# A two-layer decode kernel: other pairs stay on the chip between the layers, attention loops that run to each layer's end with the softmax ahead of the values, and the constants loaded from another queue

## The chip, the cores and the metric

One core of a Trainium2 chip runs the whole program in one launch. The metric is the device time of one execution in microseconds (us). Five executions of the kernel before took 525.45 to 526.99 us, median 525.98 us.

The core has a matrix engine (PE; its weight loads are listed as PEld), a vector engine (DVE), a scalar engine (ACT) and a queue engine (SP) that issues transfers. Sixteen DMA engines carry every transfer from HBM into the on-chip memory. "Granted clock" is the share of full speed that PE was allowed.

## The reference

Two layers, each an attention over one query token and a gated MLP, with the same weights and the same key and value caches in both layers. Only the last 4096 positions of the caches are read (W below).

```python
x = x + A(layernorm(x)); x = x + B(layernorm(x))     # twice

def A(x):                    # 32 heads of 192, D = 640, W = 4096
    q = x @ wq               # 640 x 6144
    scores = q . k * 192 ** -0.5          # per head: 4096 scores
    o = softmax(scores) @ v
    return o @ wo            # 6144 x 640

def B(x):                    # F = 1536
    return (sigmoid(x @ w_gate) * (x @ w_up)) @ w_down
```

All inputs are bfloat16. Both layers read the same 32 heads of keys and values, so what stays on the chip at the end of the first layer need not be loaded again for the second.

## The kernel before, in words

**Units.** The heads are worked on in 16 pairs. For each pair there are two units of 3552 KB (28416 bytes on each of 128 partitions): unit A holds the pair's columns of wq and its keys, unit B its values and its rows of wo. The tile `big` has seven slots of one unit each (`NSLOT = 7`) and behind them a region for MLP weights, `mreg`. `A_SLOT[l][p]` and `B_SLOT[l][p]` say in which slot the units of pair p lie in layer l. The code counts layers from 0; in this text layer 1 is `l == 0` and layer 2 is `l == 1`.

**What stays.** `KEPT` lists the units that are not released at the end of layer 1: A and B of pairs 13, 14, 15, and A of pair 12. Layer 2 starts with these pairs. Pair 12's values are loaded a second time into `mreg` (items `va`, `vb`, `vc`), and its rows of wo (`wo12`) over its own A slot once `Q(12)` has read it. The other twelve pairs, 0 to 11, are loaded again.

**Order of loads.** `seq` is the list of all loads in the order in which SP issues them: A0, A1, B0, A2, B1, ... The last B unit of a layer is cut into three pieces (`b1`, then two `b0`). A load is written down by `prefetch()` as soon as its slot is free at that point of the program (`take`, `release`), and it waits on the chip for the last reader of that slot. SP works them off strictly in order. A slot of A is released after `QK`, a slot of B after `PVout`. In layer 1 the pairs 0 to 13 rotate through slots 0 to 3; slots 4, 5 and 6 are first used for pairs 14 and 15. The first transfer on SP is the small tile of constants and x (`cst`, item `x`).

**One step.** `step(p, prev)` works on the scores of pair p and the values of the pair before:

- `Q`: 15 small matmuls form the query (L350), DVE masks it into `qs` (L353).
- `QK`: 24 matmuls give the scores (L365).
- `soft`: DVE takes the maximum (L375), ACT spreads it into `diag` (L378), PE transposes and spreads it (L381), DVE forms the bias (L382, L384). The argument `mid` puts other work between `diag` and L381.
- `PVmm`: 32 matmuls of e with the values (L419), and two copies on ACT (L424).
- `PVout`: transposes (L434), the scaling on DVE (L437), 15 matmuls with wo (L444).
- `expo`: ACT computes e and its sum (L389). `ET`: e is transposed (L395, L399) and the reciprocal of the sum is formed (L400, L402, L404).

The order of PE before is Q, QK, PVmm(prev), L381, PVout(prev), ET. Each engine works in the order in which the operations are written down (`pg.op`). PE's part of steps 1 to 12 of layer 1 and of steps 2 to 9 of layer 2 is a loop on the chip whose body is two steps (`loop`); the other steps are written out. `emit_pe` builds the loop: a wait of the body counts up by a fixed number per turn. In the kernel before, the thresholds must fit exactly from the second turn on.

**MLP.** Layer 1's MLP loads gate and up weights into `mreg` in parts (`wg`, `u1`, `u2`), then the down weights (`d1`, `d2`) over parts that have been read, then `va`, `vb`, `vc`. Layer 2's MLP weights (`fg`, `fu`, `fd`) go to `mreg`, `U_SLOT` and `D_SLOT`; `finish` ends the program.

Of the kernel before, what the change touches and what calls it, by code (L numbers as in the profile page):

```python
# [17 lines left out]
NPAIR = H // 2  # L18
# [26 lines left out]
class _Prog:  # L45

    def __init__(self):
        self.ops = {e: [] for e in ("pe", "dve", "act", "pool", "dma")}
        self.cnt = {e: 0 for e in ("pe", "dve", "act", "pool")}
        self.dcnt = {}  # L50
        self.seg = None

    def op(self, eng, fn, rd=(), wr=(), ex=(), multi=False):
        d = {}

        def add(ev):
            if ev is not None and d.get(ev[0], 0) < ev[1]:
                d[ev[0]] = ev[1]
        for r in rd:
            add(r.w)  # L60
        for r in wr:
            if r.w is not None and r.w[0] != eng:
                add(r.w)
            for ev in r.rd:
                if ev[0] != eng:
                    add(ev)
        for r in ex:
            for e, ev in r.last.items():
                if e != eng:
                    add(ev)  # L70
        if eng == "pe":
            d.pop("pe", None)
            multi = True
        self.cnt[eng] += 1
        ev = (eng, self.cnt[eng])
        for r in rd:
            r.rd.append(ev)
        for r in wr:
            r.w = ev
            r.rd = []  # L80
        for r in ex:
            r.last[eng] = ev
        self.ops[eng].append(dict(fn=fn, deps=d, multi=multi, seg=self.seg))
        return ev

    def dma(self, fn, sem, wr=(), extra=()):
        d = {}

        def add(ev):
            if ev is not None and d.get(ev[0], 0) < ev[1]:  # L90
                d[ev[0]] = ev[1]
        for r in wr:
            for ev in r.rd or [r.w]:
                add(ev)
        for ev in extra:
            add(ev)
        self.dcnt[sem] = self.dcnt.get(sem, 0) + 16
        ev = ("d:" + sem, self.dcnt[sem])
        for r in wr:
            r.w = ev  # L100
            r.rd = []
        self.ops["dma"].append(dict(fn=fn, deps=d, sem=ev[0]))
        return ev
# [3 lines left out]
def decode_kernel(ctx: ExitStack, tc: tile.TileContext, cx: bass.AP, ua: bass.AP, ub: bass.AP,  # L107
# [75 lines left out]

    A_SLOT = [{p: p % 2 for p in range(NPAIR)}, {p: 3 if p % 2 == 0 else 2 for p in range(NPAIR)}]
    B_SLOT = [{p: 2 + p % 2 for p in range(NPAIR)}, {p: 5 if p % 2 else 0 for p in range(NPAIR)}]
    A_SLOT[0].update({14: 4, 15: 6})
    B_SLOT[0].update({14: 5, 15: 2})
    A_SLOT[1].update({0: 1, 1: 4, **{p: A_SLOT[0][p] for p in (12, 13, 14, 15)}})
    B_SLOT[1].update({0: 6, **{p: B_SLOT[0][p] for p in (13, 14, 15)}})
    KEPT = {(k, p) for p in (13, 14, 15) for k in "ab"} | {("a", 12)}  # L190
    U_SLOT, D_SLOT = 1, 4
    NHALF = NB * DH // 2
# [10 lines left out]
    seq += [("wg", 0), ("wg", 1), ("u1",), ("u2",), ("d1",), ("d2",), ("va",), ("vb",), ("vc",)]  # L203
    tail = stream(1, range(12))
    assert tail[0] == ("a", 1, 0)
    seq += [("a0", 0), ("a0", 1), ("wo12",)] + tail[1:]
    seq += [("fg",), ("fu",), ("fd", 0), ("fd", 1), ("fd", 2)]
    seq_pos = [0]
    busy = set()
    ev_done = {}  # L210
    halves = {(0, NPAIR - 1), (1, 11)}
    A0CUT = WQE + W
# [11 lines left out]
    def try_load(it):  # L224
# [17 lines left out]
        elif k == "a0":  # L242
            if f"a13_{it[1]}" not in ev_done:
                return False
            s = A_SLOT[1][0]
            o0, o1 = ((0, A0CUT), (A0CUT, UNIT))[it[1]]
            pg.dma(q_dma(slot(s, o0, o1 - o0), ua[0][:, o0:o1]), f"a0{it[1]}", wr=[res(f"a0{it[1]}")] + ([rslot[s]] if it[1] else []),
                   extra=[ev_done[f"a13_{it[1]}"]])
        elif k == "wg":
# [16 lines left out]
        elif k in ("va", "vb", "vc"):  # L266
            if "down0" not in ev_done:
                return False
            o0, o1 = MOFF[k[1]]
            pg.dma(q_dma(mreg(o0, o1 - o0), ub[12][:, o0:o1]), k, wr=[rm[k[1]]])  # L270
        elif k == "wo12":
            if "Q12" not in ev_done:
                return False
            pg.dma(q_dma(slot(A_SLOT[1][12], 0, WOE), ub[12][:, VE:UNIT]), "wo12", wr=[res("wo12")], extra=[ev_done["Q12"]])
        elif k == "fg":
# [23 lines left out]

    pg.dma(q_dma(cst[:, 0:CE], cx), "x", wr=[res("cst")])  # L300
    prefetch()
# [35 lines left out]
    def attention(l, xi):  # L337
# [6 lines left out]
        def Q(p, y):  # L344
            sa = A_SLOT[l][p]

            def f(t):
                for i, c0 in enumerate((0, P, 2 * P)):
                    for c in range(DC):
                        ins = t.matmul(qe[:, i:i + 1], lhsT=slot(sa, c * 2 * DH + c0, P), rhs=xq[:, c:c + 1], start=(c == 0), stop=(c == DC - 1))  # L350
                return ins
            ev = pg.op("pe", f, rd=[res("xq"), rslot[sa]] + ([res("a00")] if l == 1 and p == 0 else []), ex=[rb[3]])
            pg.op("dve", lambda v: v.tensor_tensor(out=qs[:, y], in0=qe[:, 0:3].unsqueeze(2).to_broadcast([P, 3, 32]), in1=mask3, op=ALU.mult),  # L353
                  rd=[res("cst")], wr=[res(f"qs{y}")], ex=[rb[3]])
            return ev

        def QK(p, y, x=0, ks=(0, 1, 2)):
# [3 lines left out]
            def f(t):  # L361
# [5 lines left out]
                return ins  # L367
            ev = pg.op("pe", f, rd=[res(f"qs{y}"), rslot[sa]] + ([res("a00"), res("a01")] if l == 1 and p == 0 else []), ex=sc_x[3:5])
            if ks[-1] == 2 and not (l == 0 and ("a", p) in KEPT) and not (l == 1 and p in (12, 13)):
                release(sa)  # L370
# [36 lines left out]
        def PVmm(p, z):  # L407
            inm = l == 1 and p == 12
            sv = None if inm else B_SLOT[l][p]
# [17 lines left out]
        def PVout(p, z):  # L427
            inm = l == 1 and p == 12
            sv = None if inm else B_SLOT[l][p]

            def tm(t):
                for c in range(3):
# [5 lines left out]
                  rd=[res(f"Rn{z}0"), res(f"Rn{z}1")], wr=[res("oTb")], ex=[rb[6]])  # L438
            wo = slot(A_SLOT[1][12], 0, WOE) if inm else slot(sv, VE, WOE)

            def im(t):
# [4 lines left out]
                return ins  # L446
            sa = A_SLOT[1][12]
            pg.op("pe", im, rd=[res("oTb")] + ([res("wo12"), rslot[sa]] if inm else [rslot[sv]]), ex=[rb[7]])
            if inm:
# [7 lines left out]

        def step(p, prev, y=0):
            Q(p, y)
            QK(p, y)  # L460
            soft(0, hook=None, mid=lambda: PVmm(prev, prev % 2))
            PVout(prev, prev % 2)
# [9 lines left out]
        if l == 0:  # L472
# [6 lines left out]
            ET(0)  # L479
            loop(0, 12)  # L480
            first, n = 12, NPAIR
        else:
            Q(13, 0)
            ln_sq(xi)
            mark("a13_0", QK(13, 0, ks=(0,)))
            mark("a13_1", QK(13, 0, ks=(1, 2)))
            Q(14, 1)
            ln_rstd(K2_ATT, eps_a, srs_c, res("srs"))
            mark("Q12", Q(12, 0))
            QK(14, 1, 1)  # L490
            soft(0, scale_pm)
            expo()
            ET(0)
            Q(15, 1)
            soft(1)
            expo(1)
            QK(15, 1)
            soft(0, mid=lambda: PVmm(13, 0))
            PVout(13, 0)
            ET(1)  # L500
            expo()
            PVmm(14, 1)
            ET(0)
            QK(12, 0)
            PVout(14, 1)
            soft(0, mid=lambda: PVmm(15, 0))
            PVout(15, 0)
            expo()
            ET(1)
            Q(0, 0)  # L510
            QK(0, 0)
            soft(0, mid=lambda: PVmm(12, 1))
            PVout(12, 1)
            expo()
            ET(0)
            step(1, 0)
            loop(1, 8)
            first, n = 9, 12
        for p in range(first, n - 1):
            step(p + 1, p)  # L520
        PVmm(n - 1, (n - 1) % 2)
        PVout(n - 1, (n - 1) % 2)
        return residual(xi)
# [113 lines left out]
    def emit(name, h, lo=0, hi=None, known=None):  # L637
        known = {} if known is None else known
        for o in pg.ops[name][lo:hi]:
# [7 lines left out]
            if att is not None:  # L647
                ins._wait_ge(S[att[0]], att[1])
            ins.then_inc(S[o["sem"]], 16) if name == "dma" else ins.then_inc(S[name], 1)
        return known  # L650

    def emit_pe(t):
        ops, known, i = pg.ops["pe"], {}, 0
        tmp = t.alloc_register("thr_tmp")
        while i < len(ops):
# [27 lines left out]
            for (p, k), d in vals.items():  # L683
                base[p, k] = max(v - it * step_of(p, k) for it, v in d.items())
                assert all(base[p, k] == v - it * step_of(p, k) for it, v in d.items() if it), ("wait threshold is not affine", p, k, d)
                if len(set(v - it * step_of(p, k) for it, v in d.items())) > 1:
                    print("first differs", seg, p, k, d, base[p, k])
            for it in range(len(its)):
# [21 lines left out]

    NFIRST = 3
    known_sp = emit("dma", nc.sync, 0, NFIRST)
    with nc.Block() as block:
        @block.sync
# [80 lines left out]
```

## Time and profile before

| | |
|---|---|
| median of five executions | 525.98 us |
| the profiled execution, whole | 525.18 us |
| its span, first to last instruction | 523.3 us |
| mean granted clock of PE | 0.592 |
| busy: PE, DVE, ACT | 280.4, 96.0, 87.9 us |
| read from HBM | 219.18 MB, 419 GB/s over the span |

A page of the profile cuts the span into 40 slices of 13.08 us and gives the DMA engines' busy share in tenths and their rate in GB/s for each. A chain of waits follows the work that ended last back to the start. A timeline lists instructions: start, duration, engine, line, what is written and read, and in brackets the idle time ahead of it with what ended it. A row of the windows gives, for a stretch of the span, each engine's busy time with the number of instructions, then the granted clock, the DMA share and the rate. The groups of PE's waits, each with total time, number of times and the longest, in us:

```profile
PE o L419 <- DMA big<-in_ub_dram: 110.1, 24, 5.0
PE bank L350 <- DMA big<-in_ua_dram: 46.0, 23, 8.8
PE bank L395 <- ACT e_sb L389: 21.4, 30, 2.0
PE bank L444 <- DVE sh L437: 15.2, 32, 0.6
PE bank L381 <- ACT diag L378: 3.5, 3, 2.0
```

Behind the page lie the trace's records of single DMA packets: start, duration, size and queue of each. One row of a unit, 28416 bytes, is one packet, and each of the 16 DMA engines carries 8 of a unit's 128 rows. When an engine has finished its share, it writes 4 bytes to the load's semaphore, so 16 such writes mark a load's landing; the time from the first to the last of them tells how far the engines are apart.

### The profile page before, as it was taken

The numbers are of one execution on the slowest core, as the hardware profiler recorded it, in microseconds if no ns is written. First come the engines' busy times: TensorE is split into PE (matmuls) and PEld (weight loads), VectorE is DVE, ScalarE is ACT, GpSimd is POOL, SyncE is SP. The second block draws the span as 40 slices with busy tenths as digits, with TensorE's granted clock in tenths as the row PEclk, the third lists the DMA queues.
The fourth block names the chain that finished last, engine by engine and source line by source line (L and its number), as shares of the span: only waits on it lengthen the run. The fifth ranks groups of instructions, "written<-read, shape, count | busy, mean of one in ns | idle before, by whom it ended". The sixth has DMA issues, their size and how long they took to land.

```text
span 523.3 us, 8405 instructions
## 1 busy us (share of the span) xinstructions
PE 280.4 (54%) x3716; PEld 144.8 (28%) x3716; DVE 96.0 (18%) x372; ACT 87.9 (17%) x171; POOL 0.2 (0%) x4
## 2 busy tenths in 40 slices
PE   0635455544635354544655668788455544645375
PEld 0222122212322122212224434444222212322234
DVE  1211121112111121112111232223121112111121
ACT  0121021201121021201121022312121201121120
POOL 0000000000000000000000000000000000000000
PEclk9995555555556655766665556766655555556655
DMA  8999999999999999999999999999999999999995
GB/s 350 421 440 426 434 428 432 434 426 434 428 434 431 430 432 430 434 430 431 427 411 370 366 434 437 425 434 431 426 430 432 433 432 430 428 433 429 420 424 220
DMA packets 11118, 219.50 MB, mean 419 GB/s; under 512 B 1368, under 2 KB 1368, under 8 KB 2904
## 3 DMA queue, kind: packets, MB, share of 16 engines
q1 hardware_dynamic: 11096, 219.19, 98.4%
q8 instruction: 16, 0.26, 0.2%
q14 instruction: 6, 0.05, 0.0%
HBM read 219.18 MB, written 0.00 MB: 419 GB/s over the span
## 4 chain that ended last, share of the span: by engine, by line
DMA 75%; PE 18%; DVE 3%; SPq 1%; ACT 1%; issue 1%; ACTq 0%; DVEq 0%
DMA big<-in_ub_dram 59%; DMA big<-in_wu_dram 8%; PE o L419 8%; DMA big<-in_wd_dram 8%; PE scores L365 3%; PE bank L381 2%; PE bank L444 2%; SPq L182 1%; ACT e_sb L389 1%; DVE sc L382 1%; PE bank L402 1%; PE bank L350 1%; DVE sc L384 1%; PE o L365 1%; DVE sc L375 0%
## 5 line engine op out<-in xcount | busy, mean ns | idle before, releaser
L419 PE MATMUL o<-big,et_sb 128*2 128x384 bf16 x1024 | 85.4, 510 | 110.1 <-DMA big<-in_ub_dram 110.1
L365 PE MATMUL scores<-big,qs 128*32 128x512 bf16 x744 | 85.3, 630 | 10.3 <-DVE qs L353 9.8
L419 PEld LDWEIGHTS o<-big,et_sb 128*2 128x2 bf16 x1024 | 29.7, 115 | 168.1 <-DMA big<-in_ub_dram 132.2
L375 DVE TENSOR_REDUCE sc<-scores 128x1 f32<-128x1024 f32 x31 | 37.9, 1224 | 82.0 <-PE scores L365 82.0
L424 ACT CAST o_sb<-o 128x384 bf16<-128x384 f32 x64 | 30.5, 478 | 132.9 <-PE o L419 132.9
L378 ACT ACTIVATE diag<-cst,sc 128x128 f32<-128x128 bf16 x32 | 12.8, 402 | 223.6 <-DVE sc L375 202.1
L350 PE MATMUL bank<-sh,big 128*128 128x1 bf16 x480 | 17.8, 166 | 46.5 <-DMA big<-in_ua_dram 46.0
L389 ACT ACTIVATE e_sb<-scores,sc 128x1024 bf16<-128x1024 f32 x31 | 37.3, 1204 | 25.0 <-DVE sc L384 23.1
L382 DVE TENSOR_REDUCE sc<-bank 128x2 f32<-128x128 f32 x32 | 9.3, 292 | 175.1 <-PE bank L381 175.1
L365 PEld LDWEIGHTS scores<-big,qs 128*32 128x32 bf16 x744 | 24.4, 136 | 45.8 <-issue 33.6
L350 PEld LDWEIGHTS bank<-sh,big 128*128 128x128 bf16 x480 | 15.9, 106 | 49.5 <-DMA big<-in_ua_dram 47.9
L444 PE MATMUL bank<-sh,big 128*128 128x1 bf16 x480 | 17.6, 166 | 15.2 <-DVE sh L437 15.2
L381 PE MATMUL bank<-diag,sc 128*128 128x128 f32 x64 | 23.3, 462 | 3.5 <-ACT diag L378 3.5
L402 PE MATMUL bank<-sc 128*128 128x2 f32 x64 | 17.2, 338 | 14.5 <-DVE sc L400 14.5
L395 PE MATMUL bank<-cst,e_sb 128*128 128x8 bf16 x256 | 11.8, 169 | 21.4 <-ACT e_sb L389 21.4
L381 PEld LDWEIGHTS bank<-diag,sc 128*128 128x128 f32 x64 | 14.8, 288 | 22.5 <-ACT o_sb L424 17.3
L444 PEld LDWEIGHTS bank<-sh,big 128*128 128x128 bf16 x480 | 14.9, 102 | 17.8 <-DVE sh L437 17.3
L402 PEld LDWEIGHTS bank<-sc 128*128 128x128 f32 x64 | 14.4, 281 | 17.3 <-DVE sc L400 17.3
L353 DVE TENSOR_TENSOR qs<-bank,cst 128x96 bf16<-128x96 f32 x32 | 8.2, 258 | 55.8 <-PE bank L350 55.7
L399 DVE CAST et_sb<-bank 128x64 bf16<-128x64 f32 x32 | 7.2, 225 | 52.4 <-PE bank L395 52.4
L395 PEld LDWEIGHTS bank<-cst,e_sb 128*128 128x128 bf16 x256 | 9.1, 102 | 25.0 <-ACT e_sb L389 24.3
L404 DVE RECIPROCAL sc<-bank 64x1 f32<-64x1 f32 x64 | 10.6, 166 | 21.2 <-PE bank L402 20.1
(60 smaller groups left out, 95.9 us busy)
## 6 DMA issues: line engine op xcount, KB each, us to landing
big<-in_ua_dram SPq DMA_DIRECT2D x27, 3552.0 KB, 30.0
big<-in_ub_dram SPq DMA_DIRECT2D x26, 3552.0 KB, 28.9
big<-in_ub_dram SPq DMA_DIRECT2D x2, 2016.0 KB, 25.5
big<-in_ub_dram SPq DMA_DIRECT2D x4, 768.0 KB, 27.7
big<-in_ua_dram SPq DMA_DIRECT2D x1, 2048.0 KB, 11.6
big<-in_wg_dram SPq DMA_DIRECT2D x1, 1920.0 KB, 24.0
big<-in_wu_dram SPq DMA_DIRECT2D x1, 1920.0 KB, 28.1
big<-in_ua_dram SPq DMA_DIRECT2D x1, 1504.0 KB, 8.4
```

The source lines that it names most:

```text
L350: ins = t.matmul(qe[:, i:i + 1], lhsT=slot(sa, c * 2 * DH + c0, P), rhs=xq[:, c:c + 1], start=(c == 0), stop=(c == DC - 1))
L365: ins = t.matmul(sc_x[1 + b][32 * j:32 * j + 32, :], lhsT=qs[:, y, k, :], rhs=slot(sa, WQE + k * W + (4 * b + j) * 512, 512), start=(k == ...
L375: pg.op("dve", lambda v: v.reduce_max(out=mx, in_=sc_x[0][:], axis=AX.X), wr=[res("mx")], ex=sc_x[3:5])
L378: pg.op("act", lambda a: a.mul(out=diag[:], in_=ident, mul=mx), rd=[res("cst"), res("mx")], wr=[res("diag")])
L381: pg.op("pe", lambda t: t.matmul(dmx[:, 0:P], lhsT=ones_f, rhs=diag[:], start=True, stop=True), rd=[res("diag"), res("ones")], ex=[rb[2]])
L382: pg.op("dve", lambda v: v.tensor_reduce(out=nb2, in_=dmx[:, 0:P].rearrange("p (a r) -> p r a", r=2), axis=AX.X, op=ALU.max, negate=True), ...
L389: pg.op("act", lambda a: a.activation(out=e_sb[:], in_=sc_x[0][:], func=ACT.Exp, bias=nbias, scale=srs_c, accum_out=rowsum), rd=[res("nbia ...
L395: ins = t.matmul(qe[:, 0:2 * NB].rearrange("p (r x) -> p r x", r=2)[:, :, 4 * b:4 * b + 4], lhsT=e_sb[:, b * P:(b + 1) * P], rhs=sel, star ...
L402: pg.op("pe", lambda t: t.matmul(dmx[:, P:P + 2], lhsT=ones_f, rhs=rs2, start=True, stop=True), rd=[res("rs2"), res("ones")], ex=[rb[2]])
L419: ins = t.matmul(o8[h][32 * j:32 * j + 2, 0:2 * DH].rearrange("p (a d) -> p a d", a=2), lhsT=et_sb[:, z, h * NB + 2 * u:h * NB + 2 * u + 2 ...
L424: pg.op("act", lambda a, h=h: a.copy(out=o8_sb[:, :, h * DH:(h + 1) * DH], in_=o8[h][:, 0:2 * DH].rearrange("p (a d) -> p a d", a=2)), wr= ...
L444: ins = t.matmul(yT[:, j:j + 1], lhsT=wo[:, c * D + j * P:c * D + (j + 1) * P], rhs=oTb[:, c:c + 1], start=False, stop=(c == 2), skip_grou ...
```

## The change

- **Slots.** The units A0, B0 and A1 get slots of their own in layer 1 (4, 5, 6) and stay there. All other pairs rotate through slots 0 to 3 to the layer's end. Kept for layer 2 are A and B of pairs 0, 14, 15, and A of pair 1, which takes the part that pair 12 had (`PM = 1`). Layer 2 works on pairs 14, 15, 0, 1 and then 2 to 13.
- **Steps.** `step` has a new order: Q, QK, the whole of `soft`, `expo`, then PVmm(prev), ET, PVout(prev). The old order is kept as `packed` for the first two steps after the kept pairs of layer 2.
- **Loops.** Layer 1: step 1 written out, then the loop over steps 2 to 15. Layer 2: steps 2 and 3 written out as `packed`, then the loop over steps 4 to 13. After each loop only the values of the last pair remain.
- **Constants.** The transfer of the constants and x is issued by ACT, before its table load, instead of being SP's first.
- **Thresholds.** A wait in a loop may now be for a later event than it needs, as long as that event was written down before it.

```diff
-    A_SLOT = [{p: p % 2 for p in range(NPAIR)}, {p: 3 if p % 2 == 0 else 2 for p in range(NPAIR)}]
-    B_SLOT = [{p: 2 + p % 2 for p in range(NPAIR)}, {p: 5 if p % 2 else 0 for p in range(NPAIR)}]
-    A_SLOT[0].update({14: 4, 15: 6})
-    B_SLOT[0].update({14: 5, 15: 2})
-    A_SLOT[1].update({0: 1, 1: 4, **{p: A_SLOT[0][p] for p in (12, 13, 14, 15)}})
-    B_SLOT[1].update({0: 6, **{p: B_SLOT[0][p] for p in (13, 14, 15)}})
-    KEPT = {(k, p) for p in (13, 14, 15) for k in "ab"} | {("a", 12)}
-    U_SLOT, D_SLOT = 1, 4
+    A_SLOT = [{p: p % 2 for p in range(NPAIR)}, {p: 5 if p % 2 else 2 for p in range(NPAIR)}]
+    B_SLOT = [{p: 2 + p % 2 for p in range(NPAIR)}, {p: 3 if p % 2 else 6 for p in range(NPAIR)}]
+    A_SLOT[0].update({0: 4, 1: 6})
+    B_SLOT[0].update({0: 5})
+    A_SLOT[1].update({2: 0, 3: 1, **{p: A_SLOT[0][p] for p in (0, 1, 14, 15)}})
+    B_SLOT[1].update({2: 4, **{p: B_SLOT[0][p] for p in (0, 14, 15)}})
+    KEPT = {(k, p) for p in (0, 14, 15) for k in "ab"} | {("a", 1)}
+    PM = 1
+    U_SLOT, D_SLOT = 0, 1
...
-    tail = stream(1, range(12))
+    tail = stream(1, range(2, 14))
...
-    halves = {(0, NPAIR - 1), (1, 11)}
+    halves = {(0, NPAIR - 1), (1, 13)}
...
-    pg.dma(q_dma(cst[:, 0:CE], cx), "x", wr=[res("cst")])
+    pg.dma(q_dma(cst[:, 0:CE], cx), "x", wr=[res("cst")], q="adma")
...
-        def step(p, prev, y=0):
-            Q(p, y)
+        def step(p, prev):
+            Q(p, 0)
+            QK(p, 0)
+            soft()
+            expo()
+            PVmm(prev, prev % 2)
+            ET(p % 2)
+            PVout(prev, prev % 2)
+
+        def packed(p, y, prev):
             QK(p, y)
-            soft(0, hook=None, mid=lambda: PVmm(prev, prev % 2))
+            soft(0, mid=lambda: PVmm(prev, prev % 2))
             PVout(prev, prev % 2)
             expo()
             ET(p % 2)
...
-            loop(0, 12)
-            first, n = 12, NPAIR
+            step(1, 0)
+            loop(1, 14)
+            p = NPAIR - 1
         else:
-            Q(13, 0)
+            Q(14, 0)
...
-            step(1, 0)
-            loop(1, 8)
-            first, n = 9, 12
-        for p in range(first, n - 1):
-            step(p + 1, p)
-        PVmm(n - 1, (n - 1) % 2)
-        PVout(n - 1, (n - 1) % 2)
+            Q(2, 0)
+            packed(2, 0, PM)
+            Q(3, 0)
+            packed(3, 0, 2)
+            loop(3, 10)
+            p = 13
+        PVmm(p, p % 2)
+        PVout(p, p % 2)
...
-                assert all(base[p, k] == v - it * step_of(p, k) for it, v in d.items() if it), ("wait threshold is not affine", p, k, d)
+                assert all(base[p, k] + it * step_of(p, k) <= its[it][p]["past"].get(k, 0) for it in range(len(its))), ("wait for what comes later", p, k, d)
...
     known_sp = emit("dma", nc.sync, 0, NFIRST)
+    emit("adma", nc.scalar)
```

In layer 2's start the pairs 13, 14, 15, 12, 0, 1 of the listing before become 14, 15, 0, 1, 2, 3, at the same places; `va`, `vb`, `vc` load pair 1's values and `wom` its rows of wo.

## The prediction

> **What bounds the kernel now.** I read the page first, then the chain of waits, the timeline at four places (start, end of layer 1's attention, the catching up in the middle of the span, the end), short windows around the first MLP, and the trace's records of single DMA packets.
>
> ```profile
> span 523.3 us, 8405 instructions
> DMA  8999999999999999999999999999999999999995
> GB/s 350 421 440 426 434 428 432 434 426 434 428 434 431 430 432 430 434 430 431 427 411 370 366 434 437 425 434 431 426 430 432 433 432 430 428 433 429 420 424 220
> q1 hardware_dynamic: 11096, 219.19, 98.4%
> q8 instruction: 16, 0.26, 0.2%
> ```
>
> The 16 DMA engines are busy in every slice; the rate sags only in slice 0, in slices 20 to 22 and in the last. The chain names many things, but read it as a clock:
>
> ```profile
> 64.31 2.73 PE o L419 x32
> ...
> 69.08 28.93 DMA big<-in_ub_dram
> 98.05 2.73 PE o L419 x32
> ```
>
> Two pairs take 98.05 - 64.31 = 33.74 us, and carry four loads of 3552 KB: 14.55 MB / 33.74 us = 431 GB/s, the plateau. A value load lands 28.9 us after its issue although it streams only 8.43 us, so about three loads stand queued and PE waits for the newest. In the plateau no engine but the DMA counts. The end is a transfer too:
>
> ```profile
> 519.33 0.47 PE o L612 x6
> 519.81 0.32 DVE o_sb L616
> ```
>
> These come after the last piece of the down weights. Time can thus be won or lost in four ways only: when the first byte flows, how many bytes flow, the hole around the first MLP, and how late the slowest of the 16 engines is.
>
> **Bytes.** Before, layer 1 loads 16 + 16 units, layer 2 loads 12 + 12 and the values of pair 12: 57. After, it is 32, then pairs 2 to 13 (24) and the values of pair 1: 57 again. Cost 0. The kept pairs change from 12 to 15 into 0, 1, 14, 15; seven units are issued at the start instead of three, but the engines are fed without a gap before too, and from pair 2 on the same four slots rotate (0 to 3). Cover: the queue of about three loads. Cost 0.
>
> **Constants on ACT's queue.**
>
> ```profile
> 0.95 0.40 SPq L182 DMA_DIRECT2D cst<-in_cx_dram  x1
> 1.41 0.88 SPq L182 DMA_DIRECT2D big<-in_ua_dram  x2
> ...
> 16.71 0.26 ACT L328 ACTIVATE sc<-bank,sc 128x1 f32<-128x1 f32 x1 [14.53 <-PE bank L327]
> ```
>
> SP's first large load moves up by 1.41 - 0.95 = 0.46 us. The packet records put the constants' 128 packets at 1.96 to 2.39 us and the first large packets from 2.46. The small packets remain (8 per engine at about 27 ns, 0.22 us), so the gain is between 0 (they still go first) and 0.46 (they hide). The large packets' first round is slow anyway (1.5 to 2.1 us against 1.05), which hides most: I take -0.35. On ACT the issue delays the table load by some 0.4 us; its first work is at 16.71, after 14.53 us idle. SP's other queued loads all move up by the same amount and are covered.
> The constants now share each engine with A's packets. If the two alternate, they end after 8 x 1.05 = 8.4 us, near 10.5 us; the chain from them to xq takes 3.86 - 2.78 = 1.1 us, and Q(0) starts at 12.49. Cost 0, with the cover nearly used up.
>
> **Softmax ahead of values.** Before, PE ran QK, values, the maximum's matmul, output, then exp and the transposes of e. Now the maximum's matmul (L381) stands ahead of the values (L419), and L395/L402 behind them. In the plateau the keys land 8.4 us before the values, so max (1.23), diag (0.40), L381 (0.80), three small DVE operations (0.5) and exp (1.4), 4.3 us, fit under the wait of 4.77 us for values. What is queued behind the moved operations: output (L434, L444) and with it the release of the value slot. Before it came 4.74 us after the values' landing (30.57 to 35.31). After: 2.73 values, 0.36 L395, 0.45 DVE, 0.58 L402, 0.32 L434, 0.32 DVE, 0.56 L444 = 5.3. SP issues 0.6 us later into a queue three loads deep: 0.
> In layer 2's catching up PE is the slower side and has no such cover. A step took 359.15 - 349.48 = 9.67 us; after, 0.56 + 0.34 + 2.75 + 1.8 (max and diag, now exposed) + 0.59 + 2.73 + 0.36 + 0.45 + 0.58 + 0.32 + 0.32 + 0.56 = 11.4. The first loop step starts as before, so its value slot comes free at about 360.3, not 357.34. Then the load ahead still streams until 366.6 (8.43 us per load): 6 us left. Two steps of 11.4 leave PE 2.3 us behind the third's keys (369.93), and it has caught up by that step's values (378.36). Cost 0; 6 us of cover are what would have to vanish.
>
> **The end of layer 1's attention**, where the order could pay.
>
> ```profile
> 266.74 2.73 PE L419 MATMUL o<-big,et_sb 128*2 128x384 bf16 x32 [4.78 <-DMA big<-in_ub_dram]
> ...
> 272.87 0.38 PE L402 MATMUL bank<-sc 128*128 128x2 f32 x2 [0.45 <-DVE sc L400]
> 273.18 1.95 PE L419 MATMUL o<-big,et_sb 128*2 128x384 bf16 x24
> ...
> 275.33 0.81 PE L419 MATMUL o<-big,et_sb 128*2 128x384 bf16 x8 [0.20 <-DMA big<-in_ub_dram]
> ```
>
> PE gets to pair 15's values at 273.18; the last quarter starts at 275.33, when its piece lands. With the new order PE is there at 266.74 + 5.3 = 272.1, but the last quarter still starts at the landing. Gain 0 (at most the 0.20 us, if the landing moves). What follows, and so the hole, is the same:
>
> ```profile
> 280.00:284.00 4.00, 2.59 (x72) 2.42 (x72) 0.61 (x3) 0.73 (x3) 0.00 (x0) 0.50 0.92 319
> 292.00:296.00 4.00, 3.04 (x54) 2.23 (x58) 0.90 (x8) 0.00 (x0) 0.00 (x0) 0.50 0.88 310
> ```
>
> Against 431 the four windows from 280 to 296 lose about 1.0 + 0.8 + 0.7 + 1.1 = 3.6 us. Their order of issue is renamed, not moved. At the end of layer 2 PE likewise gains, and the gate then waits for its weights (1.11 us idle before at 509.96): 0.
>
> **Loops to the layer's end.** Unrolled steps before: 13, 14, 15 and 0, 1, 10, 11; after: 1 and 2, 3. Four steps of 104 matmuls and 104 weight loads are no longer in the code. Where code runs straight, PE's instruction packets (16 KB, 0.9 to 1.1 us, one engine each) came at 315.07, 324.64, 336.21, 346.88, one per 10.6 us or 1.1 steps; so 3 or 4 of the 16 go. Each puts one engine back by some 0.5 us (the data packet beside it took 0.47 to 0.55 us more than 1.05). The completions show it: the 16 engines finish the first two loads within 0.66 us of each other, the later ones of layer 1 within 1.9, those of layer 2 within 2.5, 2.9 from 363 us, and 3.2 at 496. A load counts when its slowest engine is done. Two of the packets that go (473.51, 493.19) lie where the spread grew from 2.9 to 3.2. Bounds: -0.75 (the growth 2.5 to 3.2 goes, and no new one hits) to +0.5 (one packet falls on the latest engine). I take -0.3.
> Layer 1's loop now ends right ahead of pair 15's values. The loops' ends of before bound this:
>
> ```profile
> 468.90 0.59 PE L402 MATMUL bank<-sc 128*128 128x2 f32 x2 [0.45 <-DVE sc L400]
> 471.15 0.56 PE L350 MATMUL bank<-sh,big 128*128 128x1 bf16 x15 [1.66 <-DMA big<-in_ua_dram]
> ```
>
> Leaving a loop took at most 1.66 us, all of it under the wait for keys; the entry at 349.36 shows 0.12 us of issue. PE is ready at 272.1 and needs 1.95 us before 275.33: 1.28 us of room. Cost 0 to 0.4; I take 0.
> The Trainium skill speaks against this: "Runtime: NRT & Kernel Launch", section "Instruction fetch mechanics", says that a taken branch breaks the sequential prefetch, that a target outside the window must be fetched first, and that kernels therefore prefer to be unrolled. The packet records show no PE instruction packet between 54.9 and 237.08, through five returns to the loop's head: here the loop stays loaded. By the rule the change would lose a fetch per return or at the end of the loop; by the row it loses nothing.
>
> **Sum.** -0.35 - 0.3 = -0.65 us. The profiled execution took 525.18 (span 523.3 and 1.9 around it), 0.8 under the median; on it 524.5, on the median 525.98 - 0.65 = **525.3 us**. All lower ends: -0.46 - 0.75 - 0.2 = -1.4, and -2.6 if layer 1's spread goes too; upper: +0.5 + 0.4 = +0.9.
>
> **Rivals.** What this kernel's measurement tells from no change is 0.2%, 1.05 us.
> *The spread goes in layer 1 too, faster.* The spread jumps from 0.66 to 1.8 us with the packet at 27.53, and pair 15's landing, which starts the MLP, carries it. If the shifted packets miss the late engine, that landing is up to 1.2 us earlier. For: the code's pages shift by a step. Against: a packet there remains. With half of it, the whole 0.46 and the layer 2 growth halved: -0.6 - 0.46 - 0.4 = -1.5, 524.5 us. Chance 0.40.
> *The loop's end stalls, slower.* If the code behind layer 1's loop isn't there, PE waits a jump's 0.65 us (54.25 to 54.9), a packet of 1.05 and some 0.5 to land, 2.2 us, or twice that for two pages. From 1.28 us on, it delays pair 15's values, the gate and every load behind it: +0.9 to +3.1, middle +2.0; with -0.3, 527.7 us. For: the place has hardly any cover. Against: both old ends show none beyond 1.66. Chance 0.13.
> *The constants starve* behind seven loads (59 us): PE begins near 61, slots come free some 20 us late, about 546 us. Against: instruction packets of another queue get through within 1.1 us amid full load. Chance 0.02.
> *Nothing of size happens*: my forecast, 0.45, own range 524.9 to 526.2.
>
> **How the numbers follow.** Faster 0.40, same 0.45, slower 0.15. The range 524.0 to 526.6 leaves out the extreme of the spread and the longer stalls, about 0.2.
>
> **What would show it.** Right: first keys issued near 0.95; 57 units; rate by slice as before; pair 15's last quarter waiting for its landing, with more idle time ahead of it; 12 or 13 PE instruction packets. Wrong: slices 20 to 22 shallower or deeper, Q(0) later than its keys, a DMA share under 0.95 in 300 to 380 us, or a gap on PE named issue at the end of layer 1's loop.

## The result, and the profile after

| | before | after |
|---|---|---|
| median of the executions | 525.78 us (46) | 524.55 us (26) |
| range of the executions | 524.45 to 527.37 | 523.13 to 526.18 |
| ratio, 95% interval | | 0.9978 (0.9971 to 0.9986) |
| the profiled execution, whole | 525.18 us | 524.30 us |
| its span | 523.3 us | 522.5 us |
| 16 KB packets of PE's code in it | 16 | 13 |

The change makes the kernel 1.23 us faster, 0.22%, with an interval of 0.14 to 0.29%. The profiled executions differ by 0.88 us. Single executions of one kernel lie up to 3 us apart, so no single profile proves a difference of this size; the medians do, and the profiles tell where to look.

The head of the page of the changed kernel, with the rate by slice of 13.06 us and the queues:

```profile
span 522.5 us, 8445 instructions
GB/s 351 433 434 430 434 419 435 435 429 437 422 434 437 424 437 426 431 437 426 433 412 374 366 434 436 430 425 436 423 431 436 424 435 431 431 435 424 424 427 221
q1 hardware_dynamic: 10952, 219.13, 98.4%
q8 instruction: 13, 0.21, 0.2%
q10 hardware_dynamic: 144, 0.06, 0.1%
```

The rates are those of before, within 12 GB/s in every slice: the same start (351), the same hole around the first MLP (412 374 366, before 411 370 366), the same end. The constants now go through a queue of their own, q10. PE's code (q8) takes three packets fewer.

The start, from the timeline of the changed kernel (start, duration, engine, line, what):

```profile
0.90 0.40 ACTq L182 DMA_DIRECT2D cst<-in_cx_dram  x1
0.95 0.87 SPq L182 DMA_DIRECT2D big<-in_ua_dram  x2
...
6.82 0.17 DVE L308 TENSOR_SCALAR sc<-cst 128x2 f32<-128x2 bf16 x1 [4.54 <-DMA cst<-in_cx_dram]
...
12.54 0.56 PE L351 MATMUL bank<-sh,big 128*128 128x1 bf16 x15 [4.84 <-DMA big<-in_ua_dram]
```

The first keys are issued 0.46 us earlier, and yet Q(0) starts at 12.54, not earlier than the 12.49 of before. The constants, which were there at 2.78 us, are there at 6.82: by the packet records their 128 packets no longer all go ahead of the keys', and the last of them ends at 5.41 us instead of 2.41.

The end of layer 1's attention:

```profile
266.84 2.73 PE L420 MATMUL o<-big,et_sb 128*2 128x384 bf16 x32 [2.22 <-DMA big<-in_ub_dram]
...
271.89 0.82 PE L420 MATMUL o<-big,et_sb 128*2 128x384 bf16 x16
...
273.55 0.81 PE L420 MATMUL o<-big,et_sb 128*2 128x384 bf16 x8 [0.84 <-DMA big<-in_ub_dram]
275.43 0.81 PE L420 MATMUL o<-big,et_sb 128*2 128x384 bf16 x8 [1.07 <-DMA big<-in_ub_dram]
```

PE reaches pair 15's values at 271.89, 1.3 us earlier than before, and then waits 0.84 and 1.07 us for pieces: the last quarter starts at 275.43, before at 275.33. The end, in the chain of waits:

```profile
518.57 0.46 PE o L617 x7
519.03 0.02 issue
519.06 0.33 DVE o_sb L621
```

That is 0.76 us earlier than before (519.33). So the layer-1 half gains nothing in this pair of profiles, and the layer-2 half 0.8 us. What differs there are the landings. From the trace's records, the time at which the last of the 16 DMA engines finished a load, and in brackets the time since the first of them did (a0 is the first keys unit that layer 2 loads again, in two pieces):

```
load (last engine, spread)    before          after
first keys                    12.45 (0.63)    12.49 (1.08)
third load (B0)               30.52 (1.81)    30.13 (1.84)
seventh                       64.26 (1.81)    64.41 (2.40)
last piece of pair 15        275.28 (1.88)   275.39 (2.40)
second piece of a0 (a01)     309.31 (2.50)   309.13 (2.57)
load at 370                  369.88 (2.83)   369.58 (2.81)
load at 479                  479.78 (3.13)   479.24 (2.83)
load at 496                  496.73 (3.22)   496.10 (2.83)
last piece of down weights   519.28 (3.34)   518.53 (2.78)
```

In layer 2 the first engine finishes at nearly the same times (496.73 - 3.22 = 493.51 and 496.10 - 2.83 = 493.27), but before, the spread grows by 0.36 us with the code packet at 362.6 us, by 0.25 with that at 473.5 and by 0.08 around that at 493.2. The records don't name the engine; who moved is read from the sorted completions, as the value that is gone and the one that is new. By that reading an engine moved by 1.5 us at each of the three code packets, and became the last one at the first two. Around 493.2 the new last one had moved by 0.71, the step of the 8 KB code packets on q14 (the queue on which GpSimd's code shows up below), of which one came at 491.3. The changed kernel has no code packet on q8 from 366.5 to 513 us.

### The profile page after: what moved, and what is told of

Read it like the earlier page. It is cut to its first block, busy times and chain, and to the rows that moved or that the text cites. A ratio compares the mean times of both kernels' runs of the same rounds, so it can differ in the third digit from the quotient of the medians.

```text
span 522.5 us, 8445 instructions
## 1 busy us (share of the span) xinstructions
PE 275.8 (53%) x3716; PEld 140.7 (27%) x3716; DVE 98.0 (19%) x372; ACT 87.9 (17%) x171; POOL 0.2 (0%) x4
## 3 DMA queue, kind: packets, MB, share of 16 engines
HBM read 219.18 MB, written 0.00 MB: 419 GB/s over the span
## 4 chain that ended last, share of the span: by engine, by line
DMA 73%; PE 18%; DVE 4%; issue 1%; SPq 1%; ACT 1%; ACTq 0%; DVEq 0%
DMA big<-in_ub_dram 61%; PE o L420 8%; DMA big<-in_wd_dram 7%; DMA big<-in_wu_dram 5%; PE scores L366 3%; PE bank L403 2%; PE bank L445 2%; SPq L182 1%; PE bank L396 1%; ACT e_sb L390 1%; DVE sc L405 1%; DVE et_sb L400 1%; PE bank L382 1%; DVE sc L376 1%; DVE sh L438 1%
## 5 line engine op out<-in xcount | busy, mean ns | idle before, releaser
L366 PE MATMUL scores<-big,qs 128*32 128x512 bf16 x744 | 84.0, 622 | 10.2 <-DVE qs L354 9.8
L382 PE MATMUL bank<-diag,sc 128*128 128x128 f32 x64 | 22.1, 442 | 48.0 <-ACT diag L379 48.0
L445 PE MATMUL bank<-sh,big 128*128 128x1 bf16 x480 | 17.7, 166 | 16.3 <-DVE sh L438 16.3
L445 PEld LDWEIGHTS bank<-sh,big 128*128 128x128 bf16 x480 | 15.0, 103 | 18.9 <-DVE sh L438 18.4
## 6 DMA issues: line engine op xcount, KB each, us to landing
big<-in_ub_dram SPq DMA_DIRECT2D x4, 768.0 KB, 18.6
```

The lines of the kernel that those rows point to most:

```text
L366: ins = t.matmul(sc_x[1 + b][32 * j:32 * j + 32, :], lhsT=qs[:, y, k, :], rhs=slot(sa, WQE + k * W + (4 * b + j) * 512, 512), start=(k == ...
L382: pg.op("pe", lambda t: t.matmul(dmx[:, 0:P], lhsT=ones_f, rhs=diag[:], start=True, stop=True), rd=[res("diag"), res("ones")], ex=[rb[2]])
L445: ins = t.matmul(yT[:, j:j + 1], lhsT=wo[:, c * D + j * P:c * D + (j + 1) * P], rhs=oTb[:, c:c + 1], start=False, stop=(c == 2), skip_grou ...
```

## The experiments

Theory A became, after the first four runs: the gain is the shorter code. Each packet of code holds up one DMA engine, and every load lands with its slowest engine. Its rivals: the earlier start, the new order of the step, the slots, and PE itself waiting for its code. The ratios are each against the kernel before on the same chip, where its median was 525.37 to 525.74 us. "Above the changed kernel" means above the 524.55 of the main measurement, unless said otherwise.

| kernel | PE code packets | us | ratio (95%) |
|---|---|---|---|
| constants on ACT, nothing else | 16 | 525.39 | 0.9994 (0.9982 to 1.0007) |
| changed, constants back on SP | 13 | 524.60 | 0.9982 (0.9970 to 0.9994) |
| changed, old order of the step | 13 | 524.32 | 0.9974 (0.9963 to 0.9984) |
| changed, no loops | 29 | 527.46 | 1.0033 (1.0020 to 1.0046) |
| changed, written out as before | 16 | 525.43 | 1.0004 (0.9990 to 1.0017) |
| slots alone | 16 | 525.34 | 1.0007 (0.9994 to 1.0019) |
| changed, register moves on GpSimd | 13 | 524.49 | 0.9988 (0.9976 to 1.0001) |
| changed, memsets on GpSimd | 13 | 535.87 | 1.0193 (1.0179 to 1.0208) |
| changed, layer 1 written out | 22 | 526.07 | 1.0013 (1.0003 to 1.0022) |
| changed, layer 2 written out | 19 | 525.88 | 1.0004 (0.9992 to 1.0016) |

**The constants, alone and undone.** First the kernel before with this one edit:

```diff
-    pg.dma(q_dma(cst[:, 0:CE], cx), "x", wr=[res("cst")])
+    pg.dma(q_dma(cst[:, 0:CE], cx), "x", wr=[res("cst")], q="adma")
...
+    emit("adma", nc.scalar)
```

> The kernel before with one edit: the constants and x are issued by ACT. Theory 1 (the gain is the earlier first byte, about 0.4 us, and fewer PE instruction packets, the rest): ratio to before 0.9992, some 525.4 us where before is 525.8; first key packets near 2.0 us instead of 2.46. Theory 2 (the new order of the step pays at the layers' ends): 1.0000. Theory 3 (only the spread of the 16 engines counts, by PE's instruction packets): 1.0000, since the same packets are fetched.

Then the changed kernel with the edit taken back:

```diff
-    pg.dma(q_dma(cst[:, 0:CE], cx), "x", wr=[res("cst")], q="adma")
+    pg.dma(q_dma(cst[:, 0:CE], cx), "x", wr=[res("cst")])
```

> The changed kernel with the constants and x back at the head of SP's queue. Theory 1: it gives back 0.4 us, ratio to before 0.9986. Theories 2 and 3: as the changed kernel, 0.9978.

Alone it gives 0.9994, and undone 0.9982, where the changed kernel gave 0.9978. Both intervals take in 0 as well as 0.4 us; by the medians it is worth 0 to 0.2 us, by the ratios 0.2 to 0.3, so its size isn't settled. The records suggest why not all of 0.46 arrives. In the three profiles with the constants on SP the first keys land at 12.45, 12.94 and 12.77 us, with them on ACT (eight profiles, without the memsets', where GpSimd's first extra code packet comes at 10.5 us) at 12.17 to 12.56, mean 12.39: 0.33 us are there. But at pair 15's last piece the same kernels (those with 13 or 16 packets, and the one with layer 2 written out) read 275.28, 275.67, 275.37 against 275.22 to 275.57, mean 275.34: 0.1 us is left, less than they differ among themselves.

**The old order of the step**, with everything else as changed:

```diff
         def step(p, prev):
             Q(p, 0)
-            QK(p, 0)
-            soft()
-            expo()
-            PVmm(prev, prev % 2)
-            ET(p % 2)
-            PVout(prev, prev % 2)
+            packed(p, 0, prev)
```

> The changed kernel with the old order in every step (maximum's matmul after the values, e's transposes last), loops, slots and queue as changed. Theories 1 and 3: as the changed kernel, 0.9978, since the last piece's landing decides at both layers' ends. Theory 2: the gain goes, 0.9995 to 1.0005; pair 15's last quarter would start later than its landing.

0.9974: the new order buys nothing. Its timeline at the end of layer 1's attention:

```profile
272.91 0.38 PE L403 MATMUL bank<-sc 128*128 128x2 f32 x2 [0.45 <-DVE sc L401]
273.27 2.91 PE L420 MATMUL o<-big,et_sb 128*2 128x384 bf16 x32
```

PE comes 1.4 us later than with the new order, runs through all 32 matmuls in 2.91 us, and ends at 276.18; with the new order it ends at 275.43 + 0.81 = 276.24. The last piece's landing decides in both.

**No loops.** All steps written out, the order of the work unchanged:

```diff
-                pg.seg = (l, it)
+                pg.seg = None
```

> The changed kernel with every step written out, no loop on PE. 20 more steps of code, so 17 to 20 more PE instruction packets of 16 KB (30 to 33 in all, not 13), more than one on each of the 16 engines. Theories 1 and 3: each engine is put back by some 0.5 us per packet that hits it, one or two in each layer, so +0.5 to +1.5 us on the changed kernel, ratio 0.9988 to 1.0006. Theory 2: 0.9978, the code's length doesn't matter. The rule against loops (a return to the head costs a fetch): faster than the changed kernel, under 0.9975.

527.46 us, 2.9 us above the changed kernel: more than any theory had said, with 29 code packets, one fewer than the 30 to 33 expected. The page:

```profile
span 526.6 us, 8203 instructions
DMA  8999999999999999999998999999999999999994
...
q8 instruction: 29, 0.48, 0.4%
```

Is PE waiting for its code, or are the loads late? At the end of layer 1's attention:

```profile
273.76 2.25 PE L420 MATMUL o<-big,et_sb 128*2 128x384 bf16 x24
...
277.07 0.81 PE L420 MATMUL o<-big,et_sb 128*2 128x384 bf16 x8 [1.06 <-DMA big<-in_ub_dram]
```

PE waits for the piece, as in the changed kernel, but the piece comes 1.6 us later. The records of the 16 engines' completions, in us after the first of them, show the cause one engine at a time (loads 5 and 6, 22 and 23 of this kernel):

```
5   0.00 0.12 0.21 0.22 0.23 0.28 0.29 0.32 0.41 0.48 0.52 0.70 0.77 0.80 0.85 1.94
6   0.00 0.12 0.21 0.22 0.23 0.28 0.30 0.32 0.41 0.50 0.53 0.72 0.77 0.80 1.93 2.40
22  0.00 0.22 0.26 0.27 0.75 0.77 0.79 1.44 1.73 1.75 1.84 1.93 1.98 2.04 2.23 2.39
23  0.00 0.22 0.27 0.28 0.76 0.79 0.80 1.44 1.75 1.75 1.83 1.98 2.05 2.23 2.41 3.45
```

With the packet at 50.9 us one engine, and only one, moves from 0.85 to 2.40: 1.55 us for 16 KB. The first eight packets of layer 1 move eight different values in this way, each by 1.50 to 1.55 us. The ninth, at 195.3 us, moves the engine that the first had moved, from 1.93 to 3.45, and the tenth that of the second, from 2.40 to 3.92, while half of the sixteen haven't been hit by PE's code at all. The spread reaches 3.98 us at the end of layer 1, where the changed kernel has 2.40, and pair 15's last piece lands 1.64 us later. At the end of layer 2 it is 5.2 against 2.8, and the last down weights land 4.05 us later, the 1.64 of layer 1 included.

**Written out as before.** The changed kernel with seven written-out steps, as many as the kernel before had. The theories are named anew here: A is the code packets, B the constants and the slots:

```diff
-            loop(1, 14)
+            loop(1, 12)
+            step(14, 13)
+            step(15, 14)
...
-            loop(3, 10)
+            loop(3, 8)
+            step(12, 11)
+            step(13, 12)
```

> The changed kernel with as many steps written out as before: 14 and 15 of layer 1 and 12 and 13 of layer 2 besides 1, 2 and 3. Theory A (each 16 KB packet of PE's code puts one of the 16 engines back by about 1.5 us, each time another, and a load lands with its slowest engine; so the loops brought most of the gain): 16 or 17 PE instruction packets, ratio to before 0.9985 to 0.9998. Theory B (the constants' earlier start and the slots brought it, the loops little): 0.9975 to 0.9982.

1.0004: the gain is gone, with constants, order and slots as changed. On the same chip the changed kernel itself (below, with register moves that left no trace) took 524.49, this one 525.43: 0.94 us for four steps of code. The intervals of these two ratios overlap; that of this kernel and that of the main measurement (0.9971 to 0.9986) don't. The middle lies a little above the upper end of theory A's range, 0.9998, and above all of theory B's. The time shows this, the profile doesn't: it fell on this kernel's fastest execution, 523.16 us, whose last down weights landed at 517.38 us, earlier than in the changed kernel's profile (518.53). The scatter of single executions is larger than what three packets cost.

**Slots alone.** The changed kernel with that edit, the constants back on SP and the old order:

> The changed kernel with only the slots and the kept pairs as changed: constants on SP, old order, 16 to 17 packets of PE's code, seven steps written out. Theory A: 0.9995 to 1.0005, the slots by themselves do nothing. Theory B: 0.9985 or less.

1.0007, a little above theory A's range: nothing, within the interval. The slots are what lets the loops run to the end; by themselves they bring no time.

**Code of another engine.** To take PE out of it, GpSimd, which is idle, was given code to fetch. The first try was a series of register moves:

```diff
+        @block.gpsimd
+        def _(g):
+            r = g.alloc_register("pad")
+            for i in range(6144):
+                g.reg_mov(r, 1 + i % 64)
```

> The changed kernel with 6144 register moves on GpSimd, which does no other work: 393 KB of code more through the same 16 DMA engines, and PE's program as it is. Theory A: an 8 KB packet of code put one engine back by about 0.7 us in the earlier traces, so 48 of them, three on each engine, put the slowest back by 2 us or more: ratio 1.000 to 1.004. Rival C (written-out steps cost time on PE itself, waiting for its code): PE's code is untouched, so as the changed kernel, 0.9978; by the bytes alone 393 KB at 431 GB/s, +0.9 us, 0.9995.

This one failed as an experiment. The profile has GpSimd busy for 0.2 us and not one packet of code more (13 on q8, 6 on q14): as far as the profile shows, the moves were not in the program that ran. It counts as a second measurement of the changed kernel: 524.49 us, but with a ratio of 0.9988 (0.9976 to 1.0001), 0.88 us below the kernel before on this chip, less than the 1.23 of the main measurement. The second try used work that stays, one-element memsets into a tile that nothing reads:

```diff
+    scr = sb("scr", [P, 8], FP32)
...
+        @block.gpsimd
+        def _(g):
+            for i in range(3072):
+                if i and i % 32 == 0:
+                    g.wait_ge(S["pool"], i)
+                g.memset(scr[32 * (i % 4):32 * (i % 4) + 1, i // 4 % 8:i // 4 % 8 + 1], 0.0).then_inc(S["pool"], 1)
```

> The changed kernel with 3072 one-element memsets on GpSimd into a small tile that nothing reads: 197 KB of code of another engine through the same 16 DMA engines, PE's program as it is. Theory A: some 24 packets of 8 KB, each of which put one engine back by about 0.7 us in the earlier traces, one or two on each engine: the slowest is 0.7 to 1.4 us later, ratio to before 0.9992 to 1.0010. Rival C (written-out steps cost time on PE itself): as the changed kernel, 0.9975 to 0.9988; by the bytes alone +0.45 us, 0.9987 to 0.9995.

535.87 us: 11.3 us slower than the changed kernel, some ten times what theory A had said, for 197 KB of code that does nothing for the result. Its page, and short windows at the end of layer 1 (width, busy time of PE, PEld, DVE, ACT and GpSimd with instructions, granted clock, DMA share, GB/s):

```profile
span 532.4 us, 11517 instructions
DMA  8999999999999999999994999999999999999993
q8 instruction: 13, 0.21, 0.2%
q14 instruction: 30, 0.25, 0.1%
```

```profile
276.00:280.00 4.00, 2.99 (x51) 1.80 (x43) 0.92 (x5) 0.96 (x2) 2.48 (x28) 0.50 1.01 422
280.00:284.00 4.00, 3.00 (x37) 0.61 (x34) 0.00 (x0) 0.48 (x1) 2.51 (x28) 0.50 0.24 99
284.00:288.00 4.00, 2.44 (x54) 2.04 (x51) 0.93 (x9) 0.48 (x1) 2.50 (x28) 0.50 0.07 27
```

The DMA share of 0.07 is the reading to remember: one engine of sixteen is 0.0625. From 284 to 288 us one engine works off what it owes, fifteen stand still, and the whole MLP waits for it. DVE and ACT are as busy as in the changed kernel (98.0 and 87.9 us in both), so the memsets don't slow the other engines' work. The records show the same engine falling back by about 0.65 us with each of GpSimd's 8 KB packets, one every 18.6 us: the spread is 3.69 at the tenth load, 5.64 at the sixteenth, 6.99 at the twenty-second, 10.33 at the thirty-first, while the second-latest engine stays at 2.6. PE's code, in the kernel without loops, went round eight engines; GpSimd's extra code went to one. That is why the forecast, which spread the packets over sixteen engines, was so far too low.

**One layer at a time.** The loop of layer 1 or of layer 2 written out:

```diff
-                pg.seg = (l, it)
+                pg.seg = (l, it) if l == 1 else None
```

> The changed kernel with layer 1's loop written out and layer 2's kept. Theory A: 10 more PE packets, 23 in all; the landing of pair 15's last piece is 1.0 to 1.7 us later (in the kernel without loops 277.0, not 275.4) and that passes to the end: ratio 0.9998 to 1.0015. If the hole around the MLP swallowed it: 0.998.

```diff
-                pg.seg = (l, it)
+                pg.seg = (l, it) if l == 0 else None
```

> The changed kernel with layer 2's loop written out and layer 1's kept. Theory A: 7 or 8 more PE packets, 20 or 21 in all, the spread of the engines in layer 2 grows from 2.8 to 4 us or more: +0.7 to +1.7 us on the changed kernel, ratio 0.9992 to 1.0012. Rival C: 0.9978 to 0.999, since PE waits for transfers from 370 us on and has room for its code.

Both cost time: 526.07 and 525.88 us, 1.5 and 1.3 above the changed kernel, and together about the 2.9 of both. They have 22 and 19 code packets, each one less than the least expected. With layer 1 written out pair 15's last piece lands at 277.02 with a spread of 3.90, as in the kernel without loops (277.03), and the hole around the MLP does not swallow it. With layer 2 written out the spread is 3.9 at the end instead of 2.8, and the last down weights land at 519.35 instead of 518.53. Rival C falls here: the interval, 0.9992 to 1.0016, lies above the 0.9978 to 0.999 that it gave. PE's idle time between 370 and 500 us shows the same: its largest groups are those of the changed kernel (21.6 us for keys in both, 19.1 against 18.3 us for values), and none is a wait for code.

No experiment beat the changed kernel; the one with the old order (0.9974) can't be told from it.

## Why the prediction was right, and what was mis-sized

The forecast was 525.3 us, 0.65 faster; it became 524.55, 1.23 faster, inside the range of 524.0 to 526.6. Of the two cases that shared most of the chance, the forecast's own ("nothing of size happens", own range 524.9 to 526.2) was too small, and the "faster" rival's time, 524.5, was hit, but not by its mechanism: layer 1's spread did not go, it is 2.40 us in the profile after against 1.88 before, and pair 15's last piece lands at 275.39 against 275.28. That the range held the result, at a time that only the rival had given, is in part luck.

- **Bytes, kept pairs, seven loads at the start:** 0 was right. 219.18 MB in both, the slices agree, and the slots alone gave 1.0007.
- **Constants, -0.35:** the first keys do land 0.33 us earlier, and the constants come at 6.82 us, inside the bound of 10.5. In time it was 0 to 0.3 us, not clear of noise, so the runs neither confirm nor refute the size.
- **Softmax ahead of values, 0:** right at all three places. PE's idle time ahead of the last quarter grew from 0.20 to 1.07 us, as said, and its start did not move. The step in layer 2's catching up was worked out as 11.4 us; it took 356.61 - 345.19 = 11.42. The 2.3 us by which PE was to come late at the third step did not show (it waited 1.82 us there), since PE had started 4.3 us earlier; the granted clock in 300 to 304 us was 0.98 in this execution against 0.50, which may be why, but no run separates it. Neither reached the end.
- **The loop's end, 0:** right. PE entered pair 15's values 0.46 us after L445 had begun and then waited for the transfer.
- **Shorter code, -0.3:** this term was mis-sized. The mechanism, one engine put back and loads landing with the slowest, was right, and so was the count (12 or 13 packets forecast, 13 found). The weak step reads "Each puts one engine back by some 0.5 us". I had taken that from how much longer the data packet beside a code packet took. The completions give 1.5 us, three times as much, so an engine that is hit becomes the last one more often. The -0.3 itself was chosen between bounds read from the growth of the spread; of that growth the part around 493.19 was put down to PE's packet there, where the 8 KB packet at 491.3 fits better. In time the term became about -0.9 (525.43 against 524.49), with a wide margin: sixteen packets more cost 2.9 us, which gives 0.18 each and an estimate of 0.55 for three.
- **The rule weighed against it.** "Runtime: NRT & Kernel Launch", section "Instruction fetch mechanics", of the Trainium skill prefers written-out code and calls the cost of crossing a 16 KB boundary mostly hidden. In this kernel it was hidden from PE, which in the kernel without loops still waited 1.06 us for pair 15's last piece; it was not hidden from the DMA engines, which are the bound. The loops were faster by 2.9 us than the same work written out.

What stays open: why the profiled execution before loses more in layer 2 and less in layer 1 than the one after. The engine that a packet hits, and how late that engine already is, differ between kernels and executions, so single profiles scatter by about as much as one packet costs. In two of the profiles (constants alone, constants back) the spread grew by another 1.1 and 0.9 us just before the end, next to a code packet at 511.0 and 514.1 us, which moved an engine that was already late, and these two executions took 526.3 us, above their medians. In the profile after, the packet at 513.1 us moved an early engine, from 0.22 to 1.92, and the landing did not change. That this is what spreads single executions is argued, not shown.

## What to carry to other kernels

In a kernel that is bound by its transfers, an instruction stream is a transfer too: it takes few bytes, but here each packet of it held up one DMA engine, and a load split over sixteen engines lands with the slowest. Look at the spread of the engines' completions, not only at the DMA's busy share, keep long stages in loops where the loop's code stays loaded, and count the code of an engine that is otherwise idle as well. A reordering that gives an engine more room ahead of a transfer is worth nothing as long as the transfer lands last.

## What the runs showed of the hardware

- A 16 KB packet of PE's code put one DMA engine back by 1.5 us, though by its size at 431 GB/s / 16 it would take 0.6 (an estimate). In layer 1 of the kernel without loops eight packets in a row moved eight different engines, and the ninth to twelfth moved engines that had been moved before.
- GpSimd's extra 8 KB packets put one and the same engine back, by 0.65 us each: 15 of them left it 10.3 us behind by 274 us, and all 24 cost 11.3 us.
- A loop of about 420 matmuls and weight loads on PE ran its turns without one fetch between 72 and 283 us in the changed kernel.
- A small transfer on a second queue, issued beside seven large ones, came 4 us later than ahead of them on their queue (6.82 against 2.78 us).
